# Keys of two row tiles as a seven-product block, and a new order around it, in a PE-bound gated pair of linear attentions

## The chip, the cores and the metric

The kernel runs on one core of a Trainium2 chip. Five engines work side by side, each through its own list of instructions: PE (matmuls into the accumulators in PSUM), DVE and ACT (elementwise work, DVE also sums of two tensors), POOL, and SP, which here issues DMAs. They meet only through semaphores. The metric is device time in microseconds of one execution; the median of three runs of the kernel before is 176.27 us.

## The reference

One input x (2048 rows, 640 columns) goes through two linear attentions A and B with their own weights, and a gate mixes the results:

```python
def branch(x, wqkv, wo):                      # 32 heads of 20
    q, k, v = split(x @ wqkv)
    phi = lambda t: where(t > 0, t + 1, exp(t)) + 1e-6
    pq, pk = phi(q), phi(k)
    kv = einsum("bhsd,bhse->bhde", pk, v)
    z = einsum("bhsd->bhd", pk)
    num = einsum("bhqd,bhde->bhqe", pq, kv)
    den = einsum("bhqd,bhd->bhq", pq, z)[..., None] + 1e-6
    return merge_heads(num / den) @ wo
g = sigmoid((x * gate_w).sum(-1, keepdims=True))
out = g * branch(x, A_wqkv, A_wo) + (1 - g) * branch(x, B_wqkv, B_wo)
```

All tensors are bf16; sums are made in float32.

## The kernel before

**Stages.** The 2048 rows are 16 row tiles of 128, the 640 columns five chunks of 128. The work goes through these stages, each a set of PE products with elementwise work behind it:

- *K, keys.* For every tile t and branch X, `k_step` multiplies the transposed tile by X's key weights, chunk after chunk: five chunks of one 512-wide and one 128-wide matmul (lines 635 and 636), into a pair of PSUM banks. The gate's column rides along as column 640 of B. `k_post` makes phi: ACT takes exp (line 681), DVE clips it (684), and then either ACT takes a relu (693, 708) and DVE adds (699 for both branches at once, 711 for one), or DVE does relu and add in one scalar-tensor-tensor from PSUM (720). The results, pk, lie in PKS, by group of columns and by even and odd tile.
- *G.* In place of values first, the kernel forms pk-transposed times x, and folds the value weights in later (kv). A unit g of five covers two groups of columns, and the sum over rows is split into a 2x2 block product: the rows of even and odd tiles, the left and right 320 columns of x. It is done with seven products, P1 to P7, in place of eight, each over the eight pairs of tiles (line 1029). Tokens Gg.n name product n of unit g: 1 and 2 need only pk and x; 5, 6, 3, 7, 4 need sums that DVE makes ahead: the S sums over pk (`s_pair`, line 761), for four tiles at a time, and the T sums over x (`t_all`, line 786). ACT saves partial results (1058), DVE combines them (c11 and its like, 1063), and SP moves the finished halves by transposing DMAs (`move`).
- *Q and R, queries* (`qu_unit` line 910, `qp_unit` line 997). The first half of the rows, and one unit of the second, again by seven products per group of columns, with weight sums (`w_sums`, 857; `w_sum3`, 868) and x sums (`x_sums`, 883); token X2 makes those of the second half. The lists QD and RD say which phi of a query is finished by one scalar-tensor-tensor of DVE in place of a relu of ACT and an add of DVE.
- *kv, w, LA, d:* kv products (1176), their fold into the output weights (`wp_burst`, 1208) with a trip through DRAM (LA loads A's), and the denominators (`den`, 1282), which go through ACT and small DMAs to scale pq.
- *S, T1, O, output* (1349, 1363, 1418): sums over pq and the folded weights, and seven products for each of eight pairs of row tiles, then stores by SP.

**Order.** Every step is recorded as an operation with its buffers. PE's order is written out by hand as the tokens of MAIN, behind the K stage, which runs through its tiles in a loop. A planner (`Sched`) then walks through time with assumed costs and, for the other engines, takes whatever operation can start first, and of those the one recorded earliest; some have fixed priorities. It gives out the slots: eight PSUM banks (a key unit takes a pair), six exp buffers `ek`, and others. What runs on the chip is the fixed order that comes out, with waits on semaphores. HOP and TURN are such assumed costs: a hop between engines, and the turn of PE between full-array products and those that use a part of the array (kv, w and d have modes 3, 2 and 1).

The K stage before ends with this loop (tiles 0 and 1 come first, in a form of their own):

```python
    for t in range(2, NT):
        k_both(t, "AB" if t in RELUB else "A")
        if t % 2:
            s_pair(t // 2)
    t_all(0, 8)
```

`s_pair` does nothing at even arguments; at 1, 3, 5, 7 it makes the sums of tiles 0 to 3, 4 to 7, 8 to 11 and 12 to 15, the last split into unit 0 and units 1 to 4.

Of the kernel before, what the change touches and what calls it, by code (L numbers as in the profile page):

```python
# [7 lines left out]
ALU = mybir.AluOpType  # L8
# [39 lines left out]
MAIN = """G0.1 G1.1 G2.1 G1.2 G3.1 G2.2 G0.2 G1.5 G0.5 G1.6 G0.6 G1.3 G0.3 G2.5 G1.7 G2.6 G0.7 G2.3 G2.7 G0.4  # L48
G1.4 Q1.1 Q0.1 Q1.5 G2.4 Q0.2 Q0.5 Q0.6 G3.2 G3.5 Q0.3 G3.6 Q0.7 Q1.6 Q1.3 G3.3 Q2.5 G3.7 Q1.7 Q2.1
Q1.2 Q0.4 Q2.2 G3.4 Q2.6 Q3.1 Q4.1 Q4.5 Q2.3 Q1.4 Q3.2 Q4.6 Q2.7 G4.1 Q2.4 Q4.2 Q3.5 Q4.3 Q4.7 Q3.6  # L50
G4.2 G4.5 Q3.7 G4.6 Q4.4 Q3.3 Q3.4 G4.7 kvA X2 G4.3 G4.4 dA0 wA0 R1B wA1 LA dB0 S1 S0
kvB R2A wB0 R1A R3B R4A wB1 T1 R4B R0.1 R0.5 R2B R3A R0.2 R0.6 O0.1 O0.5 O3.1 O2.5 R0.7
R0.3 O0.2 O3.2 O2.1 O3.5 R0.4 O0.6 O3.6 O0.3 O3.3 O2.6 O2.2 O3.7 O1.1 dA1 dB1 S2 S3 O0.7 O2.3
O2.7 O1.2 O1.6 O0.4 O1.5 O1.7 O2.4 O4.1 O5.1 O7.1 O3.4 O1.4 O4.2 O5.2 O7.2 O5.5 O6.1 O5.6 O4.5 O6.2
O6.6 O5.7 O4.6 O5.3 O6.5 O7.6 O4.3 O4.7 O7.5 O7.7 O4.4 O7.3 O6.7 O5.4 O1.3 O6.3 O6.4 O7.4"""
# [5 lines left out]
QD = ("0.0A0", "0.1A0", "0.1B0", "0.2A0", "0.2B0", "0.3A0", "0.4B0", "0.4B1",)  # L61
RD = ("A1", "B0",)
# [38 lines left out]
TURN = 100.0  # L101


class Sched:
# [16 lines left out]
    def run(self):  # L121
# [30 lines left out]
        while len(self.order) < n:  # L152
            best = None
            for e in self.ENGS:
                cand = todo[e]
                if not cand:
                    continue
                look = cand[:1] if e == "PE" else cand
                pick = None
                for o in look:  # L160
                    w = can(o, at[e])
                    if w is None:
                        continue
                    key = (w if w > at[e] + 1e-6 else at[e], o.prio, w)
                    if pick is None or key < pick[0]:
                        pick = (key, o)
                if pick and (best is None or pick[0][0] < best[0][0]):
                    best = (pick[0], pick[1], e)
            if best is None:
                raise RuntimeError("stuck: " + ", ".join(c[0].name for c in todo.values() if c))  # L170
            (w, _, _), o, e = best
            for b in o.outs:
                if b.pool and b.slot is None:
                    self.take(b, w)
            for b in o.outs:
                o.deps += b.war
            w = max(w, at[e])
            if e == "PE" and o.mode != mode:
                w, mode = w + TURN, o.mode
# [24 lines left out]
    def pick(self, b, t, skip=()):  # L204
# [15 lines left out]
        c = [(max(have[i] for i in range(s, s + b.n)), s) for s in b.at if all(i in have for i in range(s, s + b.n))]  # L220
# [83 lines left out]
def body(nc, A_x, A_wqkv, A_wo, B_x, B_wqkv, B_wo, gate_w, out, log=None):  # L304
# [64 lines left out]

    PP = {("A", 0): PQ0[:, :, :].rearrange("p (b g) s -> p g b s", b=2), ("B", 0): PKS[:, 2560:7680].rearrange("p (b g s) -> p g b s", b=2, g=NC)}  # L370
# [13 lines left out]
    OST = {"os": [PKS[:, 8192 + D * k : 8832 + D * k] for k in range(NOS)], "ot": [PKS[:, SSB + D * k : SSB + D * k + D] for k in range(NOT)]}  # L384
# [12 lines left out]
    XU = {k: PKS[:, SSB + 1024 * i : SSB + 1024 * i + 1024].rearrange("p (c s) -> p c s", c=2) for i, k in enumerate((1, 2, 4))}  # L397
    XU[5, 0], XU[5, 1] = PKS[:, 1280:1792], PKS[:, 7680:8192]
# [24 lines left out]
    def dma(q, name, dst, src, nbytes, ins=(), outs=(), after=(), issue=450.0, transpose=False, prio=None, rate=330.0):  # L423
        timing = (rate, 1500.0 if loading else 1700.0) if not transpose else (140.0, 1500.0) if loading else (1000.0, 1150.0)
# [56 lines left out]
    bxo = Buf("xo")  # L481
# [254 lines left out]

    bs1, bs2, bs3, bs4 = [{} for _ in range(4)]
# [108 lines left out]
    gtx = dma("SP", "gtx", GTX.rearrange("p (t n) -> p t n", t=8), GGX, 262144, ins=[bx], outs=[bgt], after=pk_last[-12:], issue=2500.0, transpose=True)
# [23 lines left out]
    def x_sums(p, after):  # L870
        t1, t2 = 1024 * p, 1024 * p + 512
        a11, a12, a21, a22 = [XT[:, c : c + 2, lo : lo + 512] for lo in (t1, t2) for c in (0, 2)]
        for k, in0, in1, need in (
            (1, a21, a22, ()),
            (2, a11, XU[1], (1,)),
            (5, XT[:, 4, t1 : t1 + 512], XT[:, 4, t2 : t2 + 512], ()),
            (4, a12, XU[2], (2,)),
# [5 lines left out]
                lambda e, out=XU.get((k, p), XU.get(k, a21)), in0=in0, in1=in1: e.tensor_tensor(out=out, in0=in0, in1=in1, op=ALU.subtract),  # L883
# [3 lines left out]
                after=after,  # L887
# [8 lines left out]
    def qu_unit(p, g):  # L896
# [33 lines left out]
        def post(X, h, pv, ins):  # L930
# [7 lines left out]
            home = {("B", 0): lambda: [ulast[1]], ("A", 0): lambda: [], ("B", 1): lambda: list(qpe[0]), ("A", 1): lambda: qpe[0] + pqs_op["A", 0] + pqs_op["A", 1] + fx_op[2] + ([ulast[3]] if h else [])}[X, p]()  # L938
# [23 lines left out]
        def step(n):  # L962
# [6 lines left out]
            elif n == 5:  # L969
                mm(pz, True, [(WU[1][:, c, g::5], XU[1][:, c, :]) for c in range(2)] + [(wq("B", 4), xt(4, 1))], wqs + [bwu[1], bxu[p, 1]])  # L970
                d[5] = save(s5, pz)
            elif n == 6:
                mm(px, False, [(WU[2][:, c, g::5], XU[2][:, c, :]) for c in range(2)], [bwu[2], bxu[p, 2]], [d[1]])
                d[2] = save(s2, px)
            elif n == 3:
                mm(pz, False, [(wq("B", 2 + c), XU[4][:, c, :]) for c in range(2)] + [(wq("B", 4), XU[5, p])], wqs + [bxu[p, 4], bxu[p, 5]], [d[5]])
# [12 lines left out]
    def qp_unit(X, g):  # L989
        ps, eq, rq, e2, pq = Buf("q", "ps", 2, cover=(512, 512)), Buf("eq", "eq", 2, (0, 2, 4)), Buf("rq"), Buf("eq2"), Buf("pq")  # L990
        dst = PP[X, 1][:, g, :, :]
        home = list(qpe[0]) + ([ulast[3]] + pqs_op["A", 0] + pqs_op["A", 1] + fx_op[2] if X == "A" else [])
# [31 lines left out]
    def prod(g, name, ps, reg, mov, w, first, ins, after=()):  # L1024
        for j0, j1 in ([(j, j + 1) for j in range(8)] if g == 0 else [(0, 8)]):
# [13 lines left out]
    def g_unit(g):  # L1039
# [8 lines left out]
        ekfree = pk_last[-12:]  # L1048
# [8 lines left out]
        def save(dst, ps, w, name):  # L1057
            return op("ACT", lambda e: e.activation(PT[:, dst.slot, 0:w], PS[:, ps.slot, 0:w], ACT.Copy), act_cost(w), ins=[ps], outs=[dst], after=ekfree, name=name)  # L1058
# [36 lines left out]
        def move(X, k, b):  # L1095
# [9 lines left out]
                after=[gtx] if X == "B" else [],  # L1105
# [5 lines left out]
        def step(n):  # L1111
            if n == 1:
                prod(g, "P1", px, ra1, xv(0, False), W, True, lambda j: xn(j, 0) + [bpk[one[0], 2 * j]])
                d["s1"] = save(t1, px, HC, "p1s")
            elif n == 2:
                prod(g, "P2", py, ra2, xv(1, False), HC, True, lambda j: xn(j, 1) + [bpk[one[0], 2 * j + 1]])
# [143 lines left out]
    def wp_load(X, halves, lo, hi):  # L1260
# [8 lines left out]
            after=[ulast[3]] if X == "A" else [],  # L1269
# [222 lines left out]
    qsteps = []  # L1492
    for tok in MAIN.split():
        if tok[0] == "G":
            g, n = int(tok[1]), int(tok[3])
            steps[g](n)
            if n == 4:
                if g == 0:
                    w_sums([ulast[0]])
                    x_sums(0, [ulast[0]])  # L1500
# [14 lines left out]
        elif tok == "X2":  # L1515
            x_sums(1, qpe[0] + kva)
# [60 lines left out]
```

## Time and profile before

| | |
|---|---|
| runs shown | 175.95, 176.27, 176.41 us |
| the profiled execution's own time | 176.08 us |
| its span, first to last instruction | 174.6 us |
| busy: PE, DVE, ACT, POOL | 171.1, 135.6, 114.2, 5.1 us |
| granted PE clock | 1.00 |
| K products end, first G product starts | 47.8 us |
| DVE's first idle time after the S and T sums | 60.1 us |

The profile lists busy time per engine, the chain of work that ended last, groups of instructions by line, and can be asked for an order in time, for waits, and for busy time in chosen stretches. A matmul's shown length holds its pipeline, so neighbours overlap, and what one costs in a stream is the distance from start to start. A line of a group reads: line, engine, operation, output from inputs, shape, count, busy time, mean length in ns, idle time of the engine ahead of it. An idle PE is what lengthens the span here; idle time of the others need not.

### The profile page before, as it was taken

What the parts mean: (1) busy time and instruction counts of PE and PEld (TensorE: products, weight loads), DVE (VectorE), ACT (ScalarE), POOL (GpSimd) and SP (SyncE); (2) the same over time, 40 slices, a digit from 0 to 9 for tenths busy, and PEclk for the clock granted to TensorE, in tenths of its full rate; (3) what the DMA queues carried; (4) which work ended last, traced back from release to release, by engine and by line L of the source; (5) the groups of instructions that cost most, each with busy time, mean ns of one, the idle gap of its engine ahead of it and who ended that gap; (6) DMA issues with size and microseconds to landing.
All of it is one profiled execution on the core that took longest, in us unless ns stands there. A gap on an engine that the chain in (4) does not pass through costs nothing.

```text
span 174.6 us, 3344 instructions
## 1 busy us (share of the span) xinstructions
PE 171.1 (98%) x1320; PEld 108.0 (62%) x1335; DVE 135.6 (78%) x238; ACT 114.2 (65%) x218; POOL 5.1 (3%) x16
## 2 busy tenths in 40 slices
PE   9999999999999999999999999999999999999995
PEld 5555555555577767666655666655556667777773
DVE  2275996999999755846868879999999995898342
ACT  5378888988841221648699793867899865566332
POOL 2000000000000520000000000000000000000000
PEclk9999999999999999999999999999999999999999
DMA  6979999980000083554261001467670021450135
GB/s 198 295 142 195 190 374 364 350 158 6 4 0 0 0 71 82 99 130 101 41 184 41 0 4 39 97 187 185 243 188 18 0 75 33 92 192 0 38 122 179
DMA packets 33035, 20.59 MB, mean 118 GB/s; under 512 B 18260, under 2 KB 32892, under 8 KB 33020
## 3 DMA queue, kind: packets, MB, share of 16 engines
q1 hardware_dynamic: 32062, 19.76, 44.3%
q10 hardware_dynamic: 958, 0.63, 1.1%
q8 instruction: 10, 0.16, 0.4%
q14 instruction: 5, 0.04, 0.1%
HBM read 10.88 MB, written 4.26 MB: 87 GB/s over the span
## 4 chain that ended last, share of the span: by engine, by line
PE 90%; DVE 6%; ACT 2%; issue 1%; DVEq 0%
PE ps L1418 22%; PE ps L635 19%; PE ps L1029 19%; PE ps L910 12%; PE ps L997 9%; PE ps L636 6%; PE ps L562 1%; DVE WVA L1223 1%; ACT EQ L940 1%; DVE PKS L883 1%; PE ps L1282 1%; PE ps L1208 1%; PE ps L575 1%; DVE WKW L1063 1%; ACT PQ L943 1%
## 5 line engine op out<-in xcount | busy, mean ns | idle before, releaser
L635 PE MATMUL ps<-WKW,XT 128*128 128x512 bf16 x154 | 43.2, 382 | 0.0
L636 PE MATMUL ps<-WKW,XT 128*128 128x128 bf16 (+1 forms) x160 | 35.2, 220 | 0.3
L635 PEld LDWEIGHTS ps<-WKW,XT 128*128 128x128 bf16 x160 | 15.7, 98 | 19.1 <-DMA WKW<-in_A_wqkv_dram 0.3
L681 ACT ACTIVATE EKT<-ps 128x640 bf16<-128x640 f32 x32 | 22.4, 705 | 6.5 <-PE ps L636 5.8
L1029 PE MATMUL ps<-TX,PKS 128*128 128x321 bf16 (+1 forms) x160 | 23.8, 300 | 0.0
L1029 PEld LDWEIGHTS ps<-TX,PKS 128*128 128x128 bf16 x160 | 15.6, 98 | 7.2 <-DVE DEN L1077 0.3
L1029 PE MATMUL ps<-XN,PKS 128*128 128x321 bf16 (+1 forms) x120 | 17.7, 300 | 0.0
L1058 ACT ACTIVATE EKT<-ps 128x321 f32<-128x321 f32 (+1 forms) x15 | 6.4, 440 | 14.9 <-PE ps L1029 8.8
L636 PEld LDWEIGHTS ps<-WKW,XT 128*128 128x128 bf16 x160 | 15.8, 98 | 0.0
L1029 PEld LDWEIGHTS ps<-XN,PKS 128*128 128x128 bf16 x120 | 11.6, 98 | 5.2
L761 DVE TENSOR_TENSOR PKS<-PKS 128x1280 bf16<-128x1280 bf16 (+2 forms) x20 | 13.1, 686 | 0.1
L684 DVE TENSOR_SCALAR EKT<-EKT 128x1280 bf16<-128x1280 bf16 (+1 forms) x18 | 8.2, 454 | 5.9 <-ACT EKT L681 5.7
L940 ACT ACTIVATE EQ<-ps 128x512 bf16<-128x512 f32 x18 | 11.1, 614 | 2.1 <-DVE ps L924 1.4
L1063 DVE TENSOR_TENSOR WKW<-ps,EKT 128x320 bf16<-128x320 f32 x15 | 7.3, 490 | 6.4 <-PE ps L1029 5.8
L1008 ACT ACTIVATE EQ<-ps 128x1024 bf16<-128x1024 f32 x8 | 8.2, 1024 | 3.3 <-PE ps L997 2.6
L720 DVE SCALAR_TENSOR_TENSOR PKS<-ps,EKT 128x640 bf16<-128x640 f32 x12 | 9.9, 821 | 0.1
L910 PE MATMUL ps<-XT,WQA 128*128 128x512 bf16 x34 | 9.5, 379 | 0.1
L997 PE MATMUL ps<-XT,WQA 128*128 128x512 bf16 x37 | 9.0, 380 | 0.3 <-DVE PKS L1304 0.2
L997 PE MATMUL ps<-XT,WQB 128*128 128x512 bf16 x39 | 9.1, 380 | 0.2 <-issue 0.2
L693 ACT ACTIVATE PKS<-ps 128x640 bf16<-128x640 f32 x12 | 8.4, 698 | 0.0
L953 DVE TENSOR_SCALAR EQ<-EQ 128x512 bf16<-128x512 bf16 (+1 forms) x19 | 6.0, 322 | 2.7 <-ACT EQ L940 2.7
L1441 DVE TENSOR_TENSOR PKS<-ps,PKS 128x320 bf16<-128x320 f32 x8 | 3.9, 490 | 5.2 <-PE ps L1418 5.2
(155 smaller groups left out, 307.3 us busy)
## 6 DMA issues: line engine op xcount, KB each, us to landing
out_dram<-PKS SPq DMA_DIRECT2D x15, 160.0 KB, 1.8
XN<-in_A_x_dram SPq DMA_DIRECT2D x1, 2240.0 KB, 9.3
WKW<-in_A_wqkv_dram SPq DMA_DIRECT2D x5, 160.0 KB, 3.8
WKW<-in_B_wqkv_dram SPq DMA_DIRECT2D x5, 160.0 KB, 3.9
WQA<-in_A_wqkv_dram SPq DMA_DIRECT2D x1, 800.0 KB, 10.9
WQB<-in_B_wqkv_dram SPq DMA_DIRECT2D x1, 800.0 KB, 13.7
WVA<-in_A_wqkv_dram SPq DMA_DIRECT2D x1, 800.0 KB, 12.5
PKS<-in_B_wqkv_dram SPq DMA_DIRECT2D x1, 800.0 KB, 5.0
```

Of the source, the lines that this page charges most:

```text
L635: e.matmul(a[:, 0:512], l, WK[X][:, c, 0:512], start=(c == 0), stop=(c == NC - 1))
L636: return e.matmul(a[:, 512:w], l, WK[X][:, c, 512:w], start=(c == 0), stop=(c == NC - 1))
L681: op("ACT", lambda e, i=i, ps=ps: e.activation(evg(i), psg(ps), ACT.Exp), act_cost(D), ins=[ps] + first, outs=[ek, b], name="ke")
L693: op("ACT", lambda e, X=X, ps=ps: e.activation(pkt(X, t), psg(ps), ACT.Relu), act_cost(D), ins=[ps], outs=[rk], name="kr")
L720: lambda e, X=X, i=i, ps=ps: e.scalar_tensor_tensor(pkt(X, t), psg(ps), 0.0, evg(i), op0=ALU.max, op1=ALU.add),
L761: lambda e: e.tensor_tensor(out=out, in0=a, in1=b, op=ALU.subtract),
L910: r = e.matmul(PS[:, ps.slot, :], w, x, start=(first and i == 0), stop=(i == len(prs) - 1), skip_group_check=not first)
L940: o = [op("ACT", lambda e: e.activation(EQ[:, eq.slot + h, :], pv(), ACT.Exp), act_cost(512), ins=ins, outs=[eq], name="qe")]
L997: r = e.matmul(PS[:, ps.slot + h, :], WQ[X][:, c, g::5], XT[:, c, 1024 + 512 * h : 1536 + 512 * h], start=(c == 0), stop=(c == NC - 1))
L1029: r = e.matmul(PS[:, ps.slot, 0:w], reg[:, j, :], mov(j, w), start=(first and j == 0), stop=(j == 7), skip_group_check=not first)
L1063: lambda e: e.tensor_tensor(out=GT[:, dst.slot, lo : lo + HC], in0=PS[:, ps.slot, 0:HC], in1=PT[:, src.slot, 0:HC], op=ALU.add),
L1418: r = e.matmul(PS[:, ps.slot, 0:HALF], reg(g), mov(g), start=(first and g == 0), stop=(g == NC - 1), skip_group_check=not first)
```

## The change

**The block.** The keys of tiles 12 and 13 (KU = 6) of both branches become one 2x2 block product: rows are the two tiles, columns the two branches, and the sum runs over chunks 0, 1 against 2, 3 (chunk 4 is added in plain form). `ks_unit` has seven steps, K6.1 to K6.7, with 2, 3, 3, 2, 3, 2, 3 chunks for n = 1, 2, 5, 6, 3, 7, 4. It holds three pairs of banks: px, py, pz. ACT copies the first product from px to py (the fork), and saves two more into float buffers `kq`; DVE adds a saved one back in twice (`kcm`). DVE makes four weight sums ahead (`kw_sums`, 2 x 641 elements, recorded behind tile 4) and five sums of transposed x (`kx_sums`, behind tile 9). A memset on POOL makes column 640 of A's weights zero.

**Around it.** The loop over tiles stops at 9 (KT = 10). Tiles 10, 11, 14, 15 become tokens KtX, one branch of one tile each, and stand in MAIN between the block's steps; KRS lists which of these units take their relu on ACT. After the last K token, `after_k` records the sums of tiles 12 to 15 and the gate's operations, which now also wait for the last key product on PE.

**First sums in two parts.** P1 and P2 of a G unit are cut at KJ = 7: tokens 1 and 2 sum over the first seven pairs of tiles, tokens 8 and 9 over the last (tiles 14 and 15), with the save and the combine behind these.

**New order.** MAIN is new throughout. Among others, kvA and X2 stand among the Q steps, some forty tokens ahead of wA0 (X2's sums have buffers of their own and only one of them waits for kvA), dA0 comes behind wA0 in place of ahead of it, and QD and RD give DVE one more Q half and two more R units. A few buffers move (A's folded weights, the output staging), A's load of them waits for all Q steps and the last G unit, and the planner's assumed time for transposing DMAs and for one kind of turn changes.

```diff
-MAIN = """G0.1 G1.1 G2.1 G1.2 G3.1 G2.2 G0.2 G1.5 G0.5 G1.6 G0.6 G1.3 G0.3 G2.5 G1.7 G2.6 G0.7 G2.3 G2.7 G0.4
...
-G4.2 G4.5 Q3.7 G4.6 Q4.4 Q3.3 Q3.4 G4.7 kvA X2 G4.3 G4.4 dA0 wA0 R1B wA1 LA dB0 S1 S0
...
+KT = 10
+KU = 6
+KJ = 7
+KRS = ("10A", "10B", "11A", "11B", "12A", "13B", "14A", "14B", "15A", "15B", "8A", "9A", "9B",)
+MAIN = """K14A K6.1 K10A K6.2 K6.5 K6.6 K14B K6.3 K10B K6.7 K11A K11B K6.4 K15A K15B G2.1 G1.1 G2.8 G0.1 G3.1
+G1.8 G0.2 G0.8 G0.9 G1.2 G2.2 G2.9 G3.2 G0.6 G0.5 G1.9 G0.7 G3.8 G1.6 G0.3 G2.6 G1.5 G1.7 G0.4 G2.5
+G1.3 Q1.1 G2.7 G1.4 Q1.2 Q1.5 Q1.6 G3.9 G3.6 G2.3 Q1.7 Q1.3 Q0.1 Q1.4 Q4.5 Q4.1 Q0.2 Q0.6 Q0.5 G2.4
+Q4.6 Q4.2 Q0.7 kvA X2 Q0.3 G4.1 Q4.3 G4.2 G3.5 Q0.4 G4.8 Q4.7 G3.7 Q2.5 G3.3 Q2.1 G3.4 Q3.1 Q2.6
+Q2.3 G4.5 Q2.7 G4.6 Q4.4 Q2.2 G4.7 Q3.6 Q3.5 Q3.2 Q3.7 Q2.4 G4.9 G4.3 Q3.4 G4.4 Q3.3 wA0 dA0 R1A
+wA1 LA dB0 S1 S0 kvB R4A wB0 R2B R4B R1B wB1 T1 R3B R0.1 R3A R2A R0.6 R0.5 O1.1
...
+O7.2 O7.3 O7.4"""
...
-QD = ("0.0A0", "0.1A0", "0.1B0", "0.2A0", "0.2B0", "0.3A0", "0.4B0", "0.4B1",)
-RD = ("A1", "B0",)
+QD = ("0.0A0", "0.0A1", "0.1B0", "0.1B1", "0.2A0", "0.2B0", "0.2B1", "0.3A0", "1.0B1",)
+RD = ("A0", "A1", "A4", "B0",)
...
-TURN = 100.0
+TURN, TURNS = 100.0, {(1, 2): 190.0}
...
+    def kw_sums():
+        a1, a2, b1, b2 = [WK[X][:, c : c + 2, 0 : D + 1] for X in XS for c in (0, 2)]
+        for k, in0, in1, how, need in ((1, b1, a1, ALU.subtract, ()), (2, kw(1), b2, ALU.add, (1,)), (3, b1, b2, ALU.add, ()), (4, a2, kw(2), ALU.subtract, (2,))):
...
+                dve2(1282),
...
+        def step(n):
+            if n == 1:
+                mm(px, D + 1, True, [(WK["A"][:, c, :], xt(c, 0)) for c in range(2)], bx + [bwk["A", c] for c in range(2)] + [bwz])
+                d[1] = op("ACT", lambda e: e.activation(psw(py, D), psw(px, D), ACT.Copy), act_cost(D), ins=[px], outs=[py], name="kfk")
+            elif n == 2:
+                mm(py, D, False, [(WK["A"][:, c, :], xt(c, 0)) for c in range(2, 5)], bx + [bwk["A", c] for c in range(2, 5)])
+            elif n == 5:
+                mm(pz, D + 1, True, [(KW[1][:, c, :], KX[1][:, c, :]) for c in range(2)] + [(WK["B"][:, 4, :], xt(4, 1))], bx + [bkw[1], bkx[1], bwk["B", 4], bgc])
+                d[5] = save(s5, pz, D + 1)
+            elif n == 6:
+                mm(px, D + 1, False, [(KW[2][:, c, :], KX[2][:, c, :]) for c in range(2)], [bkw[2], bkx[2]], [d[1]])
+                d[2] = save(s2, px, D + 1)
+            elif n == 3:
+                mm(pz, D + 1, False, [(WK["B"][:, 2 + c, :], KX[4][:, c, :]) for c in range(2)] + [(WK["B"][:, 4, :], KX[5])], [bkx[4], bkx[5], bgc] + [bwk["B", c] for c in range(2, 5)], [d[5]])
+                comb(pz, s2, False)
+                k_post(t1, [("A", py, "%dA" % t1 in KRS), ("B", pz, "%dB" % t1 in KRS)])
+            elif n == 7:
+                mm(px, D + 1, False, [(KW[3][:, c, :], KX[3][:, c, :]) for c in range(2)], [bkw[3], bkx[3]], [d[2]])
+                d[7] = comb(px, s5, True)
+            elif n == 4:
+                mm(px, D, False, [(KW[4][:, c, :], xt(2 + c, 1)) for c in range(2)] + [(WK["A"][:, 4, :], xt(4, 1))], bx + [bkw[4], bwk["A", 4]], [d[7]])
+                for X, ps in (("B", s5), ("A", px)):
+                    k_post(t2, [(X, ps, "%d%s" % (t2, X) in KRS)])
...
-    for t in range(2, NT):
+    for t in range(2, KT):
         k_both(t, "AB" if t in RELUB else "A")
         if t % 2:
             s_pair(t // 2)
+        if t == 4:
+            kw_sums()
     t_all(0, 8)
...
+    kx_sums()
...
-            if n == 1:
-                prod(g, "P1", px, ra1, xv(0, False), W, True, lambda j: xn(j, 0) + [bpk[one[0], 2 * j]])
+            if n in (1, 8):
+                prod(g, "P1", px, ra1, xv(0, False), W, True, lambda j: xn(j, 0) + [bpk[one[0], 2 * j]], js=(0, KJ) if n == 1 else (KJ, 8))
...
-            after=[ulast[3]] if X == "A" else [],
+            after=qpe[0] + [ulast[NPU - 1]] if X == "A" else [],
...
-            x_sums(1, qpe[0] + kva)
+            x_sums(1, lambda k: kva if k == 3 else [ulast[1 if k == 5 else 2]])
```

More of the change, by code (lines that the diff above doesn't have):

```diff
@@ L219, in pick @@
             return best[0], best[4]
-        c = [(max(have[i] for i in range(s, s + b.n)), s) for s in b.at if all(i in have for i in range(s, s + b.n))]
+        c = [(max(have[i] for i in range(s, s + b.n)), s) for s in b.at if all(i in have for i in range(s, s + b.n)) and (not b.need or all(self.cover[s + i] >= b.need[i] for i in range(b.n)))]
         return min(c) if c else None
@@ new lines, in ks_unit, with xt, mm, fn @@
+    def ks_unit(j):
+        px, py, pz = [Buf("k", "ps", 2, cover=(512, 129)) for _ in range(3)]
+        py.need = (512, 128)
+        s2, s5 = [Buf("kq", "kq") for _ in range(2)]
+        d = {}
+        t1, t2 = 2 * j, 2 * j + 1
+        def xt(c, h):
+            return XT[:, c, 256 * j + 128 * h : 256 * j + 128 * h + 128]
+        def mm(ps, w, first, prs, ins, after=()):
+            def fn(e):
+                a = psw(ps, w)
+                for i, (m, l) in enumerate(prs):
+                    for lo, hi in ((0, 512), (512, w)):
+                        r = e.matmul(a[:, lo:hi], l, m[:, lo:hi], start=(first and i == 0), stop=(i == len(prs) - 1), skip_group_check=not first)
+                return r
+            kpe[:] = [op("PE", fn, len(prs) * (mm_cost(512) + mm_cost(128)), ins=ins, outs=[ps], after=after, name="K%d" % j)]
+        def save(dst, ps, w):
+            return op("ACT", lambda e: e.activation(psw(dst, w), psw(ps, w), ACT.Copy), act_cost(w), ins=[ps], outs=[dst], name="ksv")
+        def comb(ps, src, into_src):
+            return op(
+                "DVE",
+                lambda e: e.tensor_tensor(out=psw(src if into_src else ps, D + 1), in0=psw(ps, D + 1), in1=psw(src, D + 1), op=ALU.add),
+                dve1(D + 1),
+                ins=[ps, src],
+                outs=[src if into_src else ps],
+                name="kcm",
+            )
+        bx = [bxt[t1], bxt[t2]]
+        def step(n):
[21 more added lines that the diff above has]
+                    k_post(t2, [(X, ps, "%d%s" % (t2, X) in KRS)])
+        return step
@@ L1047, in g_unit @@
         W = HC + 1
-        ekfree = pk_last[-12:]
         d = {}
```

164 lines of the change are left out of this document (117 added, 47 removed).

## The prediction

> **What bounds the kernel now.** I read the busy totals first, then who waited for whom, then busy time by stage, then the order in time.
>
> ```profile
> PE 171.1 (98%) x1320; PEld 108.0 (62%) x1335; DVE 135.6 (78%) x238; ACT 114.2 (65%) x218; POOL 5.1 (3%) x16
> ...
> PE 90%; DVE 6%; ACT 2%; issue 1%; DVEq 0%
> ```
>
> PE is busy for 98% of the span, and the chain that ended last runs 90% through it. A busy PE may still wait inside its pipeline, so the list of PE's waits is asked too; these are all that it holds:
>
> ```profile
> PE ps L562 <- DVE ONE L461: 0.3, 1, 0.3
> PE ps L997 <- DVE PKS L1304: 0.2, 1, 0.2
> PE ps L997 <- issue: 0.2, 1, 0.2
> ```
>
> 0.3 us of it is the start. PE is a gapless stream, so a matmul that goes saves its whole stream time, and any new wait is paid in full. The stages (columns: length, then PE, PEld, DVE, ACT, POOL busy):
>
> ```profile
> 13.50:31.60 18.10, 17.94 (x132) 10.30 (x134) 14.48 (x24) 15.83 (x30) 0.00 (x0) 1.00 1.05 285
> 31.60:48.00 16.40, 16.29 (x121) 9.29 (x121) 15.98 (x23) 14.52 (x28) 0.00 (x0) 1.00 0.45 115
> 48.00:57.50 9.50, 9.50 (x72) 6.80 (x71) 9.13 (x19) 2.86 (x8) 0.00 (x0) 1.00 0.00 0
> 57.50:72.00 14.50, 14.45 (x104) 10.08 (x103) 9.04 (x21) 3.58 (x9) 3.88 (x4) 1.00 0.43 59
> 72.00:98.00 26.00, 25.89 (x148) 15.84 (x149) 18.01 (x41) 20.95 (x44) 0.34 (x2) 1.00 0.40 93
> 98.00:113.00 15.00, 14.56 (x240) 9.84 (x241) 13.78 (x29) 10.04 (x19) 0.00 (x0) 1.00 0.18 37
> 113.00:131.00 18.00, 17.89 (x106) 9.55 (x108) 17.79 (x27) 14.90 (x19) 0.00 (x0) 1.00 0.71 198
> ```
>
> The second is that of tiles 10 to 15: DVE 97% and ACT 89% full. The third, where DVE finishes the first sums, is as full. Granted clock 1.00 throughout.
>
> **The PE stream.** One chunk of a key product is a 512-wide and a 128-wide matmul; in the order in time they start 0.27 us apart:
>
> ```profile
> 31.76 0.38 PE L635 MATMUL ps<-WKW,XT 128*128 128x512 bf16 x1
> 31.98 0.22 PE L636 MATMUL ps<-WKW,XT 128*128 128x128 bf16 x1
> 32.03 0.38 PE L635 MATMUL ps<-WKW,XT 128*128 128x512 bf16 x1
> ```
>
> Tiles 10 to 15 are 60 chunks from 31.65 to 47.98: 0.272 each. Tiles 12 and 13 need 20 chunks now. The block product has 2+3+3+2+3+2+3 = 18. Saved: 2 x 0.272 = **0.54 us**. Splitting P1 and P2 after seven of eight pairs adds no matmul; those of Q, R, O stay.
>
> The order also swaps dA0 and wA0. Turns between full and part-array matmuls show as longer starts:
>
> ```profile
> 106.81 0.73 PE L1282 MATMUL ps<-PQ,DEN 128*32 128x256 bf16 x20
> 107.56 0.60 PE L1208 MATMUL ps<-WOA,WVA 64*60 64x320 bf16 x15
> 108.35 2.11 PE L997 MATMUL ps<-XT,WQB 128*128 128x512 bf16 x9 [0.18 <-issue]
> 110.38 0.60 PE L1208 MATMUL ps<-WOA,WVA 64*60 64x320 bf16 x15
> 110.92 0.73 PE L1282 MATMUL ps<-PKS,DEN 128*32 128x256 bf16 x20
> 111.58 1.13 PE L1176 MATMUL ps<-GSB,PKS 128*64 128x60 bf16 x55
> ```
>
> A den group followed by a wp burst takes 0.75 us to the next start (106.81 to 107.56), the one followed by kv 0.66. After the swap no den precedes a burst: **0.09 us** saved (bounds 0 and 0.12; I take the difference of the two rows). The 0.18 idle at 108.35 is one of ten matmuls missing from the records (x9), no gain. At most 0.1 more hangs on the gap at 61.87, where PE started 0.24 us later in place of 0.13; I count nothing.
>
> Sum: 0.54 + 0.09 = 0.63 us, against the profiled 176.08 (span 174.6 and 1.5 around it): 175.45. The median shown, 176.27, lies 0.19 higher: **175.64**. Everything else must hide.
>
> **DVE, key stage.** Prices: a bf16 sum of 1280 elements 0.82 (0.74 start to start when queued), of 256 0.29 (0.20), a scalar-tensor-tensor of 640 from PSUM 0.82 (0.73). Float sums from PSUM took 0.49 at 320 and 0.70 at 512, so 641 take some 0.84, 0.76 queued.
> - Four weight sums: 4 x 0.82 = 3.3 us. They need only the weights and come after tile 4 in priority; DVE idles before 31.6 by 0.71 + 0.65 + 1.42 + 0.35 + 1.42 = 4.55 us (gaps at 9.9, 12.9, 15.3, 24.1, 26.2). Five x sums, 4 x 0.2 to 0.3 and a smaller one, some 1.3 us, need transposed tiles 12, 13 and fit the last two gaps. Hidden, 0.3 us carried over. Without the gaps all 4.6 us would stand before the S sums.
> - Two combines: +1.5. Relus in place of scalar-tensor-tensors (10B, 14B, 15B in, 13A out): minus 0.7. Together +0.8 us.
> - Due work from 31.65 until the second S sum of unit 0: rest of tile 8 0.55, S sums of tiles 4 to 7 1.5, carried 0.3, tile 9 1.2, the six tiles and combines 9.35, four T sums 5.6, S sums of tiles 8 to 11 2.9, two of unit 0 0.4, two c11 0.8, waits between dependent operations 0.8 (as they now stand): 23.4, so done at 55.05. The first consumer, G0.6, comes after 8 x 0.94 + 5 x 0.134 = 8.15 us of P1 and P2, from 47.45: at 55.6. Margin **0.5 us**. Bounds: 0 (margin holds), and 1 us of stall where a 1.5 us T sum is put ahead of a due one.
>
> No trace here shows a two-source bf16 sum with odd rows; the weight sums have rows of 641. Bounds: 0.82 (the 1280 row) and, at the float rows' 1.08 ns per element, 0.70 + 770 x 1.08 = 1.53. I take 0.82, the nearest in type and size. [...]
>
> **ACT and PSUM, key stage.** ACT gets the fork into py and two saves (0.70 each, by the 640-wide rows) and two relus more: +3.5 us by durations, +3.1 at the 0.61 from start to start when queued. From tile 10 on: 25 wide operations x 0.61 + six small ones = 16 to 16.5 us against 15.8 of stage. It ends some 0.5 us later than now (48.9): about 49.5; pk of tile 15 at 50.3, first needed by G0.9 at 52.5.
> PSUM has four pairs of banks and the block holds up to three. Stepping the tokens through with these prices: K6.5 starts at 35.7, its pair (14A's) free at 35.0; K14B 37.1, pair free 36.3; K10B 39.3, py free 38.7; K11A 41.2, free 40.1; **K11B 42.53, free 42.35 to 42.45**; K6.4 43.9, combine done 42.0; K15B 46.1, free 43.7. No stall, one margin of about 0.1. Bounds: 0 to 1.6 us (below). Nothing here can gain, for the stream had no wait.
>
> **Later stages.** No DMA is added. kvA moves from 103 us to about 82. Its last transpose follows G2.3, with 7.5 us of Q and G steps between; combine, issue and landing take 0.5 + 1.2 + 2.6 = 4.3 at most with the queue free. On SP the gate's transpose (2.5 issue) stands before some moves, which the 3.2 us left cover. X2's sums, 4 x 0.69 + 0.42 + 0.82 = 4.0 us of DVE, go from 105 to 111 us, where DVE is 92% full, to the stage 72 to 98, where it idles 8 us; two more R units on DVE give 2 x (1.22 - 0.69) = 1.1 back, while ACT is spared 2 us. The A load (LA) now waits for the last Q and G steps, both issued before wA0, and for its stores after wA1 as before: zero. The last store follows O7.4 as before: zero. Edits that only loosen (relus of R's A units 0 and 1 without the first den's DMAs, X2 waiting for kvA in one sum of six) cost nothing; one more memset on POOL at the start, some 0.1 by the 5.1 us that 16 POOL operations take, lies before the first K product beside the loads; the gate's POOL sums now also wait for the last key product, 10 us before they start (58.5). Planner constants and moved buffers issue nothing.
>
> **The rivals.**
> 1. *A late sum.* DVE misses the 0.5 us margin at G0.6, or a step of the reordered 57 to 98 us. Against: about 1.5 us of slack behind G0.6. For: DVE is 97% full before. A stall of 0.1 to 1.1 us gives 175.75 to 176.75; about 176.1 at the middle.
> 2. *The other side: the pairs of PSUM.* ACT falls behind, PE waits for a pair at K11B, again at K15A. It decides once ACT needs its 0.70 us a piece instead of 0.61: 25 x 0.70 + 1 = 18.5 against 15.8 plus the 1 us it may trail, 1.7 us of stall, 176.27 - 0.63 + 1.7 = 177.3. For: margin 0.1. Against: two ACT operations in a row start 0.60 apart at 14.0 and 46.7.
> 3. *Odd rows at single rate.* 4 x 0.71 = 2.8 us that no gap holds; less 0.5 of margin, 2.3 us of stall at G0.6: 177.9.
>
> **How the numbers follow.** Forecast, no stall above 0.1 us: 0.52. Rival 1: 0.29. Rival 2: 0.13. Rival 3, with mishaps of that size elsewhere: 0.06. 0.3% (0.53 us) is about what a measurement of this kernel can tell from no change: faster is below 175.74, slower above 176.80. So faster 0.52, same 0.29, slower 0.19. The likeliest gives 175.6, its own range 175.3 to 175.8 (all turns and the gap at 61.87 gained, and noise of 0.2 as between the runs shown). The range reaches over rival 1: 175.3 to 176.8.
>
> **What would show it.** Right: 316 key matmuls in place of 320, 36 of them under the block's line; first product matmul at 47.4 to 47.5; PE's list of waits still under 1 us; weight sums at 0.82 before 17 us; no den just before a burst. Wrong: PE waiting for ACT in 35 to 46 us (rival 2), for a DVE sum at 55 to 62 (1, 3), weight sums at 1.5 (3), or a PE gap near kvA, 80 to 84, ended by a DMA.

## The result and the profile after

| | before | after |
|---|---|---|
| median | 176.29 us | 176.83 us |
| profiled execution | 176.08 us | 176.63 us |
| its span | 174.6 us | 175.2 us |

The ratio is 1.0028, 95% interval 1.0020 to 1.0036: the changed kernel is slower by 0.49 us (0.35 to 0.63). The interval leaves out 1, so the loss is clear of noise, although it is below the 0.3% that the prediction took for the least that can be told from no change. It lies on the other side of the forecast of 175.6, and the median is 0.03 us past the end of the range. One of the 22 runs of the changed kernel was slow, 257.22 us; it counts in the median and not in the ratio.

The page of the changed kernel gives the busy totals and the chain that ended last:

```profile
PE 172.1 (98%) x1331; PEld 107.6 (61%) x1331; DVE 140.3 (80%) x246; ACT 116.2 (66%) x221; POOL 4.9 (3%) x17
...
PE 94%; ACT 4%; issue 1%; DVE 0%; ACTq 0%
```

PE is as full as before. What is new is the 4% of ACT in the chain, where before it was 6% of DVE and 2% of ACT. The waits of PE in the changed kernel, all of them:

```profile
PE ps L1156 <- ACT PKS L711: 0.3, 1, 0.3
PE ps L580 <- DVE ONE L478: 0.3, 1, 0.3
PE ps L653 <- ACT GE L690: 0.2, 1, 0.2
```

The total is 0.8 us, against 0.7 before, which looks harmless. But two of these are new, one in the first key tiles (line 653) and one in the first products of G (line 1156), and the list counts a wait only from the modelled end of the matmul before. The stages of the changed kernel (length, then busy PE, PEld, DVE, ACT, POOL) point to the second:

```profile
13.50:31.60 18.10, 18.10 (x135) 10.30 (x134) 15.30 (x29) 15.45 (x30) 0.00 (x0) 1.00 1.10 275
31.60:48.00 16.40, 16.40 (x123) 9.29 (x121) 16.08 (x23) 15.47 (x29) 0.00 (x0) 1.00 0.49 127
48.00:57.50 9.50, 9.10 (x66) 6.12 (x65) 8.79 (x19) 4.71 (x10) 0.00 (x0) 1.00 0.00 0
57.50:72.00 14.50, 14.50 (x107) 10.28 (x106) 10.77 (x24) 4.10 (x10) 3.73 (x4) 1.00 0.27 51
```

The third is the only one of these four in which PE isn't full (9.10 of 9.50, before 9.50), and ACT, 2.86 us busy there before, now has 4.71: it is late.

**Where the time went.** The true measure is the distance between starts of matmuls in the order in time. Cut into four stretches at places that all kernels here share, it gives (us, by the starts as printed):

| | tile 2's first key product to the first one behind tile 9 | from there to the first G product | from there to the den group of the second half (dA1) | from there to the last matmul | sum |
|---|---|---|---|---|---|
| before | 21.77 | 16.32 | 96.16 | 28.25 | 162.50 |
| after | 22.13 | 15.79 | 96.69 | 28.25 | 162.86 |
| difference | +0.36 | -0.53 | +0.53 | 0.00 | +0.36 |

The promised saving is there, in its place: 0.53 us of the 0.54. It is given back twice: 0.36 ahead of it, 0.53 behind it. The sum starts at tile 2, since that start itself falls anywhere from 9.72 to 10.52 us in executions of kernels that do the same until then; with that, +0.36 agrees with the +0.49 (0.35 to 0.63) of the runs, at the low end of the interval.

**The first place: tile 3.** PE in the changed kernel:

```profile
12.56 0.22 PE L654 MATMUL ps<-WKW,XT 128*128 128x129 bf16 x1
12.99 0.38 PE L653 MATMUL ps<-WKW,XT 128*128 128x512 bf16 x1 [0.21 <-ACT GE L690]
```

After a narrow matmul the next starts 0.055 us on; here it is 0.43. The loss is 0.375 us, of which the bracket shows 0.21. The first key product of tile 3 waits for a pair of PSUM banks. What DVE did just before, in the changed kernel:

```profile
9.17 0.82 DVE L767 TENSOR_TENSOR GSA<-WKW 128x1282 bf16<-128x1282 bf16 x1
9.91 0.81 DVE L738 SCALAR_TENSOR_TENSOR PKS<-ps,EKT 128x640 bf16<-128x640 f32 x1
10.64 0.82 DVE L767 TENSOR_TENSOR GSA<-GSA,WKW 128x1282 bf16<-128x1282 bf16 x1
11.38 0.32 DVE L702 TENSOR_SCALAR EKT<-EKT 128x640 bf16<-128x640 bf16 x1
11.61 0.82 DVE L767 TENSOR_TENSOR GSB<-WKW 128x1282 bf16<-128x1282 bf16 x1
12.35 0.82 DVE L738 SCALAR_TENSOR_TENSOR PKS<-ps,EKT 128x640 bf16<-128x640 f32 x1
```

All four weight sums (line 767) stand among the scalar-tensor-tensors of tiles 0 and 1, each of which is the last to read a pair of banks and so frees it; three of the sums stand ahead of the third, shown last here. In the kernel before, the third began at 11.02:

```profile
11.02 0.82 DVE L720 SCALAR_TENSOR_TENSOR PKS<-ps,EKT 128x640 bf16<-128x640 f32 x1
```

It begins at 12.35 now; 0.18 of the difference is the later start of tile 2 in this trace. In the order before, tile 3 took the pair that this operation frees; the planner, with the pair late, gave it that of tile 2's branch A, which a relu of ACT frees at 12.84:

```profile
12.13 0.71 ACT L726 ACTIVATE PKS<-ps 128x640 bf16<-128x640 f32 x1
```

Either way PE waits: the other pair comes free at 13.17. The bracket names line 690, the gate's exp, but that one ends at 12.99, after the weight load of the late matmul has begun (12.96), so it is not what PE waited for.

**The second place: the start of G.** ACT in the changed kernel, end of the key stage:

```profile
45.13 0.71 ACT L699 ACTIVATE EKT<-ps 128x640 bf16<-128x640 f32 x1
45.71 0.21 ACT L690 ACTIVATE GE<-PQ 128x1 f32<-128x1 f32 x1
45.81 1.40 ACT L726 ACTIVATE PKS<-PQ 128x640 bf16<-128x640 f32 x1
47.08 1.40 ACT L699 ACTIVATE EKT<-PQ 128x640 bf16<-128x640 f32 x1
48.34 1.33 ACT L699 ACTIVATE EKT<-ps 128x640 bf16<-128x640 f32 x2
49.50 0.22 ACT L690 ACTIVATE GE<-ps 128x1 f32<-128x1 f32 x1
49.55 0.77 ACT L711 ACTIVATE PKS<-ps 128x640 bf16<-128x640 f32 x1
50.14 0.78 ACT L699 ACTIVATE EKT<-ps 128x640 bf16<-128x640 f32 x1
50.72 0.79 ACT L711 ACTIVATE PKS<-ps 128x640 bf16<-128x640 f32 x1
```

Relu and exp of unit 13B take 1.40 us each; the same operation on the same 640 floats takes 0.71 from PSUM. 13B is the one key unit whose floats lie in SBUF: the block's combine leaves them in s5, a buffer in PQ. Both kinds of read go through `psg`, which takes every fifth element (20 bytes on) to put the columns in order of groups. From start to start the two cost 1.27 and 1.26 in place of some 0.6, so the relus of 15A and 15B (line 711) end at 50.32 and 51.51. First PE at the start of G in the kernel before, in one piece, then in the changed kernel, with its weight loads, which show the second wait better:

```profile
47.81 7.80 PE L1029 MATMUL ps<-XN,PKS 128*128 128x321 bf16 x56
```

```profile
48.77 1.26 PE L1156 MATMUL ps<-XN,PKS 128*128 128x321 bf16 x8
50.37 2.32 PE L1156 MATMUL ps<-XN,PKS 128*128 128x321 bf16 x14 [0.34 <-ACT PKS L711]
...
51.56 0.52 PEld L1156 LDWEIGHTS ps<-XN,PKS 128*128 128x128 bf16 x5 [0.39 <-ACT PKS L711]
```

G0.1 starts at 50.37, right behind the first relu, G3.1 at 51.56, right behind the second: both products were given the banks that these relus free. By starts they are 0.51 and 0.225 us late, 0.735 together. Against it stand the turn (0.10) and the gap at 61.87, which is gone (0.11): 0.735 - 0.10 - 0.11 = 0.53, as in the third column of the table.

### The profile page after: what moved, and what is told of

The parts are those of the page before. It is cut to its first block, busy times and chain, and to the rows that moved or that the text cites. A ratio compares the mean times of both kernels' runs of the same rounds, so it can differ in the third digit from the quotient of the medians.

```text
span 175.2 us, 3364 instructions
## 1 busy us (share of the span) xinstructions
PE 172.1 (98%) x1331; PEld 107.6 (61%) x1331; DVE 140.3 (80%) x246; ACT 116.2 (66%) x221; POOL 4.9 (3%) x17
## 4 chain that ended last, share of the span: by engine, by line
PE 94%; ACT 4%; issue 1%; DVE 0%; ACTq 0%
PE ps L1546 22%; PE ps L1156 20%; PE ps L653 16%; PE ps L1035 13%; PE ps L1124 10%; PE ps L654 4%; ACT EKT L699 3%; PE ps L809 3%; PE ps L580 1%; PE ps L1410 1%; PE ps L1336 1%; PE ps L1304 1%; ACT PKS L711 1%; PE ps L593 1%; ACT PKS L726 0%
## 5 line engine op out<-in xcount | busy, mean ns | idle before, releaser
L653 PE MATMUL ps<-WKW,XT 128*128 128x512 bf16 x140 | 39.5, 383 | 0.2 <-ACT GE L690 0.2
L654 PE MATMUL ps<-WKW,XT 128*128 128x128 bf16 (+1 forms) x140 | 30.9, 221 | 0.0
L699 ACT ACTIVATE EKT<-ps 128x640 bf16<-128x640 f32 x31 | 21.6, 711 | 5.3 <-PE ps L654 4.8
L653 PEld LDWEIGHTS ps<-WKW,XT 128*128 128x128 bf16 x140 | 13.8, 99 | 17.2 <-issue 0.7
L1156 PE MATMUL ps<-XN,PKS 128*128 128x321 bf16 (+1 forms) x120 | 18.7, 300 | 0.4 <-ACT PKS L711 0.3
L654 PEld LDWEIGHTS ps<-WKW,XT 128*128 128x128 bf16 x140 | 13.8, 99 | 0.0
L711 ACT ACTIVATE PKS<-ps 128x640 bf16<-128x640 f32 x16 | 11.4, 711 | 0.0
L1035 PE MATMUL ps<-XT,WQA 128*128 128x512 bf16 x36 | 10.4, 379 | 0.0
L1124 PE MATMUL ps<-XT,WQA 128*128 128x512 bf16 x40 | 9.2, 381 | 0.0
L1611 ACT ACTIVATE PKS<-ps 128x320 bf16<-128x320 f32 x8 | 3.5, 437 | 8.1 <-PE ps L1546 8.1
L738 DVE SCALAR_TENSOR_TENSOR PKS<-ps,EKT 128x640 bf16<-128x640 f32 x10 | 8.2, 818 | 0.0
L1569 DVE TENSOR_TENSOR PKS<-ps,EKT 128x320 bf16<-128x320 f32 x9 | 4.4, 491 | 4.1 <-PE ps L1546 3.8
```

The source lines that it names most:

```text
L653: e.matmul(a[:, 0:512], l, WK[X][:, c, 0:512], start=(c == 0), stop=(c == NC - 1))
L654: return e.matmul(a[:, 512:w], l, WK[X][:, c, 512:w], start=(c == 0), stop=(c == NC - 1))
L699: op("ACT", lambda e, i=i, ps=ps: e.activation(evg(i), psg(ps), ACT.Exp), act_cost(D), ins=[ps] + first, outs=[ek, b], name="ke")
L711: op("ACT", lambda e, X=X, ps=ps: e.activation(pkt(X, t), psg(ps), ACT.Relu), act_cost(D), ins=[ps], outs=[rk], name="kr")
L738: lambda e, X=X, i=i, ps=ps: e.scalar_tensor_tensor(pkt(X, t), psg(ps), 0.0, evg(i), op0=ALU.max, op1=ALU.add),
L1035: r = e.matmul(PS[:, ps.slot, :], w, x, start=(first and i == 0), stop=(i == len(prs) - 1), skip_group_check=not first)
```

## The experiments

The theory after the traces: two separate causes, the weight sums early on DVE (0.36 us) and the strided reads of SBUF on ACT (0.7 us). The rivals: that both gaps are only ACT carrying more work, or that the reads are slow because the buffer is in SBUF at all, however it is read. Kernels that stand in one table shared the runs of the kernel before.

| | edit of | median | ratio to before |
|---|---|---|---|
| e1_late_w | after | 176.27 | 0.9994 (0.9981 to 1.0007) |
| e9_swap | after | 181.45 | 1.0283 (1.0266 to 1.0300) |
| e2_flat13 | after | 175.94 | 0.9972 (0.9961 to 0.9984) |
| e8_no13B | after | 176.32 | 0.9992 (0.9980 to 1.0004) |

### e1_late_w: the weight sums later

```diff
+        if t == 2:
+            kw_after = [pk_last[-1]]
...
                 ins=[bwk[X, c] for X in XS for c in range(4)] + [bgc, bwz] + [bkw[j] for j in need],
                 outs=[bkw[k]],
+                after=kw_after,
```

> The four weight sums may start only once the keys of tile 2 are done; all else is as in the changed kernel. Theory (a): the changed kernel loses 0.4 us at 12.6 because the sums stand on DVE ahead of the scalar-tensor-tensors of tiles 0 and 1, which free PSUM. Then PE goes on without the 0.38 us gap there, the first G product starts at 47.4 in place of 47.8, and the ratio to before falls from 1.0028 to about 1.0005 (176.4). Rival: the gap belongs to the start (clock, first loads) and stays; ratio 1.0028.

Measured 0.9994 against 1.0028, the expected 1.0005 within the interval. DVE in this kernel:

```profile
12.40 0.82 DVE L738 SCALAR_TENSOR_TENSOR PKS<-ps,EKT 128x640 bf16<-128x640 f32 x1
...
15.74 0.83 DVE L767 TENSOR_TENSOR GSA<-WKW 128x1282 bf16<-128x1282 bf16 x1
16.49 0.83 DVE L767 TENSOR_TENSOR GSB<-WKW 128x1282 bf16<-128x1282 bf16 x1
```

The sums come behind the last scalar-tensor-tensor of the first tiles, at the same price, and tile 3 starts without a gap: from tile 2 to the first key product behind tile 9 it takes 21.76 us, as in the kernel before (21.77). Nothing later on DVE came too late for it. The waits at the start of G stay (0.50 and 0.22 by starts), so the causes are two.

### e2_flat13: 13B read in order

```diff
         def psg(ps):
+            if ps.pool == "kq":
+                return psw(ps, D).rearrange("p (g m) -> p g m", g=NC)
             return psw(ps, D).rearrange("p (m g) -> p g m", g=NC)
```

> As in the changed kernel, but the exp and relu of tile 13, branch B, read and write in order; the permutation of its columns is left out, so keys of this tile and branch stand at the wrong columns. It tells the read's stride from the place. Theory (b): 0.70 each, no PE gap at 49 to 52, ratio about 0.9986. If reading float32 from SBUF costs 1.4 us in any order, times and gaps stay. Rival (ACT overloaded as such): gaps above 0.4 us stay.

Measured 0.9972, a little better than the 0.9986 expected, which lies outside the interval; in the traces, from tile 2 on, it is 0.75 us below the changed kernel, as expected. ACT in this kernel, and PE from the start of G:

```profile
46.35 0.75 ACT L728 ACTIVATE PKS<-PQ 128x640 bf16<-128x640 f32 x1
46.97 0.74 ACT L701 ACTIVATE EKT<-PQ 128x640 bf16<-128x640 f32 x1
...
48.35 8.47 PE L1158 MATMUL ps<-XN,PKS 128*128 128x321 bf16 x61
```

From the same buffer in SBUF, in order, 0.75 and 0.74 in place of 1.40. So it isn't SBUF as such, and it isn't the stride as such either, since the same stride in PSUM takes 0.71: what is dear is the 20-byte stride in SBUF, at 1.40. The first 61 matmuls of G run in one piece: both later waits are gone, with as many operations on ACT as in the changed kernel, so ACT was not overloaded as such. The wait of tile 3 stays (0.377 us, behind the matmul at 13.10).

### e9_swap: read in order, written with a stride

```diff
         def psg(ps):
+            if ps.pool == "kq":
+                return psw(ps, D).rearrange("p (m g) -> p m g", g=NC)
             return psw(ps, D).rearrange("p (m g) -> p g m", g=NC)
...
+        def mg(ps, v):
+            return v.rearrange("p g m -> p m g") if ps.pool == "kq" else v
...
-            op("ACT", lambda e, i=i, ps=ps: e.activation(evg(i), psg(ps), ACT.Exp), act_cost(D), ins=[ps] + first, outs=[ek, b], name="ke")
+            op("ACT", lambda e, i=i, ps=ps: e.activation(mg(ps, evg(i)), psg(ps), ACT.Exp), act_cost(D), ins=[ps] + first, outs=[ek, b], name="ke")
```

> The exp and relu of tile 13, branch B, read their float buffer in SBUF in order and write with a stride, where the changed kernel reads with a stride and writes in order. Same instructions in the same order. Theory (b): it is the strided read of float32 from SBUF that doubles these two (1.40 us each in place of 0.70), and the 1.4 us that ACT is late makes the two PE gaps at 49.7 and 51.2 (0.51 and 0.23). Then they take about 0.70, both gaps go, ratio about 0.9986. If a strided write costs the same, they stay at 1.4 and the ratio at 1.0028. Rival: ACT is late through its added operations as such (3.5 us more work); then the gaps stay above 0.4 us even at 0.70.

This was expected to mend the loss (0.9986) and made it far worse: 1.0283. ACT in this kernel, in order of time:

```profile
45.77 3.07 ACT L731 ACTIVATE PKS<-PQ 128x640 bf16<-128x640 f32 x1
48.33 3.35 ACT L704 ACTIVATE EKT<-PQ 128x640 bf16<-128x640 f32 x1
```

Neighbouring bf16 elements now go to places 256 bytes apart in the exp buffer (line 704, 3.35 us) and, by the layout of PKS, 4096 bytes apart for the relu (line 731, 3.07 us). The longest of PE's waits in this kernel, and the stretches around it (length, busy PE, PEld, DVE, ACT, POOL, granted clock):

```profile
PE ps L1161 <- ACT PKS L716: 3.5, 1, 3.5
```

```profile
50.00:54.30 4.30, 0.79 (x6) 0.59 (x7) 2.00 (x5) 4.30 (x7) 0.00 (x0) 1.00 0.00 0
54.30:57.40 3.10, 3.10 (x14) 1.53 (x13) 3.10 (x5) 1.12 (x3) 0.00 (x0) 0.51 0.00 0
57.40:64.00 6.60, 6.60 (x49) 4.70 (x48) 4.96 (x12) 1.09 (x4) 0.00 (x0) 0.97 0.00 0
```

PE waits 3.5 us for the relu of 15A, and then pays again: for 3.1 us from 54.3 on the clock is granted at 0.51, and over the 6.6 us behind at 0.97, together some 1.7 us of full clock (0.49 x 3.1 + 0.03 x 6.6). The waits of up to 0.5 us in the changed kernel left the clock at 1.00; what a wait between these lengths does is not shown.

### e8_no13B: DVE reads the stride in place of one ACT operation

```diff
-KRS = ("10A", "10B", "11A", "11B", "12A", "13B", "14A", ...
+KRS = ("10A", "10B", "11A", "11B", "12A", "14A", ...
```

> The relu of tile 13, branch B, goes from ACT to DVE (a scalar-tensor-tensor from the float buffer in place of relu and add). Theory (b): ACT is spared the 1.39 us relu, exp stays at 1.4, so ACT is late by 0.7 less than its 1.4; the gap at 49.7 falls below 0.1, that at 51.2 as well, unless the sum on DVE is slowed by the same stride: 0.82 us if not, 1.2 or more if it is. Ratio 0.999 to 1.001. Rival (ACT overloaded as such): same direction, gap smaller by up to 0.7, so this run tells prices and not the cause.

Measured 0.9992. Without 13B in the list its relu goes from ACT to a scalar-tensor-tensor of DVE. ACT and DVE in this kernel:

```profile
46.39 1.40 ACT L699 ACTIVATE EKT<-PQ 128x640 bf16<-128x640 f32 x1
...
49.03 1.31 DVE L738 SCALAR_TENSOR_TENSOR PKS<-PQ,EKT 128x640 bf16<-128x640 f32 x1
50.26 0.82 DVE L738 SCALAR_TENSOR_TENSOR PKS<-ps,EKT 128x640 bf16<-128x640 f32 x1
```

DVE pays here too, 1.31 us against 0.82 with the same stride in PSUM, 0.77 ns more an element. No run lets this operation read the buffer in order; the block's combine, which adds 641 floats read in order from such a buffer to as many from PSUM, took 0.82 to 0.83 in the changed kernel, so on DVE too the stride in SBUF is the likely cause. One slow read less on ACT shortens the waits at the start of G from 0.735 to 0.27 us. I had expected under 0.1 to be left: the exp alone still makes ACT too late.

The second set of kernels, with its own runs of the kernel before (e14_swap_d was run once, beside its profile):

| | edit of | median | ratio to before |
|---|---|---|---|
| e13_late_m129 | after | 175.67 | 0.9953 (0.9937 to 0.9970) |
| e15_w_alone | before | 176.98 | 1.0031 (1.0018 to 1.0044) |
| e14_swap_d | before | 176.82 (one run) | |

### e13_late_m129: both mends

```diff
         def psg(ps):
+            if ps.pool == "kq":
+                return psw(ps, 645).rearrange("p (g m) -> p g m", g=NC)[:, :, 0:128]
...
+        def gm(b):
+            return psw(b, 645).rearrange("p (g m) -> p g m", g=NC) if b.pool == "kq" else psw(b, 645).rearrange("p (m g) -> p g m", g=NC)
...
-                d[5] = save(s5, pz, D + 1)
+                d[5] = save_gm(s5, pz)
...
-                d[7] = comb(px, s5, True)
+                d[7] = comb_gm(px, s5)
```

and `after=kw_after`, which in e1_late_w holds the weight sums back. The save into s5 and the combine do the permutation themselves, while they read PSUM, and write five runs of 129 floats (128 columns and, in the first, the gate's); exp and relu then read s5 in order.

> Both mends at once, with every column in its place: the weight sums start after the keys of tile 2, and the save of product 5 writes its float buffer by column groups (645 columns read from PSUM with a stride, written in order), so that the combine, the exp and the relu of tile 13, branch B, go through SBUF in order. Theory (a) and (b) together: no PE gap of the three is left, so the stream's saving of 0.54 and the turn's 0.1 come through: ratio 0.9955 to 0.9970, 175.6 to 175.9 against 176.4. If the strided read of PSUM with a float32 write costs ACT more than 0.75 us, K6.3 or K11B waits. Rival (ACT overloaded as such): gaps at 48 to 52 us come back, ratio 0.998 to 1.000.

Measured 0.9953, a little beyond the expected 0.9955 to 0.9970: faster than the kernel before by 0.83 us (0.53 to 1.11). Its trace, tile 2 to the end, is 161.75 us, 0.75 below. ACT and PE in order of time, then the third stage, then all of PE's waits:

```profile
45.58 0.75 ACT L731 ACTIVATE PKS<-PQ 128x640 bf16<-128x640 f32 x1
46.20 0.74 ACT L704 ACTIVATE EKT<-PQ 128x640 bf16<-128x640 f32 x1
...
47.58 8.47 PE L1173 MATMUL ps<-XN,PKS 128*128 128x321 bf16 x61
```

```profile
48.00:57.50 9.50, 9.50 (x72) 6.84 (x70) 9.15 (x20) 3.49 (x9) 0.00 (x0) 1.00 0.00 0
```

```profile
PE ps L653 <- DMA WKW<-in_A_wqkv_dram: 0.5, 2, 0.3
PE ps L580 <- DVE ONE L478: 0.3, 1, 0.3
```

No wait is left behind the first loads, and G is one piece again. The moved permutation is free on ACT: the save took 0.729 us with the stride in PSUM, that of the other partial result, in order, 0.736. By columns it is 21.77, 15.78, 95.95 and 28.25: the 0.54 of the block, and 0.21 of turn and vanished gap.

### e15_w_alone: the sums put into the kernel before

```diff
+    op("POOL", lambda e: e.memset(WKC[:, :, 0, D : D + 1], 0.0), 100.0, outs=[bwz], name="wkz")
...
+        if t == 4:
+            kw_sums()
```

The four weight sums and the memset of a column; nothing reads them.

> The kernel before with nothing added but the four weight sums (and the memset of their column) recorded behind tile 4; nobody reads them. Theory (a): they are put ahead of the same scalar-tensor-tensors, and PE gets the gap of 0.38 us at about 12.6 with no block in the program at all: ratio 1.0015 to 1.003. Rival (the gap belongs to the block's or the start's other changes): no gap, ratio 1.000.

Measured 1.0031, and the same gap. PE in this kernel:

```profile
13.19 0.22 PE L638 MATMUL ps<-WKW,XT 128*128 128x129 bf16 x1
13.62 0.38 PE L637 MATMUL ps<-WKW,XT 128*128 128x512 bf16 x1 [0.21 <-ACT GE L674]
```

0.43 from start to start again, 0.375 lost. From tile 2 to the first key product behind tile 9 it takes 22.14 us, the rest is that of the kernel before. The sums alone (with the small memset on POOL) bring the first loss; no block is needed for it.

### e14_swap_d: the swap alone in the kernel before

```diff
-G4.2 G4.5 Q3.7 G4.6 Q4.4 Q3.3 Q3.4 G4.7 kvA X2 G4.3 G4.4 dA0 wA0 R1B wA1 LA dB0 S1 S0
+G4.2 G4.5 Q3.7 G4.6 Q4.4 Q3.3 Q3.4 G4.7 kvA X2 G4.3 G4.4 wA0 dA0 R1B wA1 LA dB0 S1 S0
```

> The kernel before with dA0 and wA0 exchanged and nothing else. The turn theory of the prediction: from the start of the first den group to the next start 0.66 us in place of 0.75, from the burst's start to the next 0.54, PE stream shorter by about 0.1 us; the time itself can't show that in one look. Rival: the longer turn has to do with the first use of a part of the array and not with the pair den, burst; then it moves to the burst.

176.82 in one run, no gain. In its trace the burst (line 1208) is followed by the den group (1282) 0.66 us on, in place of the 0.54 expected:

```profile
107.30 0.60 PE L1208 MATMUL ps<-WOA,WVA 64*60 64x320 bf16 x15
107.96 0.73 PE L1282 MATMUL ps<-PQ,DEN 128*32 128x256 bf16 x20
```

The den group waits 0.13 us there for an operation of DVE on DEN, which eats the turn. In the changed kernel DEN is ready, and the same two rows stand closer:

```profile
107.47 0.60 PE L1336 MATMUL ps<-WOA,WVA 64*60 64x320 bf16 x15
108.00 0.73 PE L1410 MATMUL ps<-PQ,DEN 128*32 128x256 bf16 x20
```

0.53. So the turn's 0.10 us is real, but it is the whole new order that earns it, not the swap. The rival, a longer turn that moves to the burst, is out: the burst starts 0.23 us behind the 320-wide matmul ahead of it, as the den group did in the kernel before. A further 0.23 of the swapped kernel's time is a wait of PE for a relu of ACT at 128.8, which the changed kernel doesn't have; the swap also moved some later operations in the planner's order, and no run tells which of them brought the wait.

## Why the prediction was wrong

By its own steps:

- **The PE stream, 0.54: right.** 280 matmuls under the tile's lines and 36 under the block's, 316 in all, and 0.53 us less from the end of tile 9 to G. The sign named for it, the first G product at 47.4 to 47.5, didn't show (47.82), because of the loss ahead of it.
- **The turn, 0.09: right.** 0.10. The gap at 61.87, counted at nothing with at most 0.1 hanging on it, went: 0.11 more, a gain outside the sum.
- **"Four weight sums ... Hidden": wrong, 0.36 us.** The sum over DVE's gaps (4.55 us of idle time against 3.3 + 1.3) was right, and proved nothing. The planner takes what can start first; a sum that needs only weights goes in as soon as DVE has nothing ready, and if that is just ahead of a scalar-tensor-tensor, it pushes it back by up to 0.82, the length of a sum. I named no operation queued behind the sums, though the view of DVE in time showed at 11.02 the one that frees tile 3's banks. e1_late_w and e15_w_alone show it from both sides.
- **ACT, "25 wide operations x 0.61": wrong, 0.735 us.** I priced by width alone. Two of the 25 read floats in SBUF with a stride, and cost 0.65 us more each, 1.3 us of lateness: ACT's last relu, of 15B, ended at 51.5, where I had 49.5. With those two in order (e13_late_m129) it ended at 49.98 in a trace whose tile 2 starts 0.31 later than before, so the rest of this sum was sized right. And pk, which I had at 50.3, wasn't the first to matter: the banks that 15A and 15B hold were needed by G0.1 and G3.1, ahead of G0.9, which I took as the first consumer. Rival 2 had engine and resource right, an ACT that falls behind and PE that waits for a pair, and place, cause and price wrong: pieces from PSUM still started 0.6 apart, K11B and K15A had no wait, and the price was 0.74 in place of 1.7.
- **Margin at G0.6, odd rows: right.** PE has no gap from 51.6 to 62, so rival 1 didn't happen. There the late start of G had given DVE 0.735 us more, but e13_late_m129, where G isn't late, has no gap either. (8 x 0.94 + 5 x 0.134 is 8.19 and not 8.15; the margin doesn't hang on it.) The price of the weight sums, 0.82, was an estimate from the row of 1280; with rows of 641 they took 0.82 each, so rival 3, whose "single rate" is the 1.08 ns an element of the float rows (1.53 for a sum), is dead.
- **Later stages at zero: right.** kvA at 83 us, X2's sums and LA bring no wait, and from dA1 on both kernels take 28.25 us. The memset on POOL was priced at some 0.1 us from 5.1 us for 16 operations, which is 0.32 each; in the trace it took 0.12 (line 499), and no wait of PE shows it.

In one line: -0.53 of stream, -0.10, -0.11, against +0.36 and +0.735, makes +0.36 in the traces. Without the two mis-sized terms it would have been -0.75, which is what e13_late_m129 shows. That the median lies only 0.03 us past the range is luck: the range was stretched to 176.8 for rival 1, which didn't happen, and two other losses filled it.

The stride is a price of the layout: elements 20 bytes apart in SBUF took 1.40 us against 0.75 in order on ACT, and 1.31 against 0.82 from PSUM on DVE. These runs show the price and not its mechanism.

What stays open: why the same stride costs ACT and DVE nothing in PSUM is not settled by these runs, only that it is so (0.71 for ACT, against 0.70 of the fork's copy in order; 0.82 for DVE, as of the combine in order). The layouts between, strides of two to four floats, were not tried.

## What to carry to other kernels

Where PE has no gaps, spare time on another engine hides an added operation only if no operation that stands behind it in the fixed order frees what PE waits for (here four sums of 0.82 us cost 0.36): look at the neighbours in time, not at the sum of the gaps. Price a copy or an activation by its operands' memory and stride, not by its width alone (here 0.71 from PSUM with the stride, 0.75 from SBUF in order, 1.40 from SBUF with the stride); when float32 columns must be permuted as here, do it at the operation that reads PSUM (0.729 us with the stride, 0.736 in order), and leave SBUF in order. A list of waits can look the same while 1.1 us are lost: compare the starts of matmuls stage by stage.

## What the runs showed of the hardware

| 640 floats to bf16 | us |
|---|---|
| ACT, PSUM, 20-byte stride | 0.71 |
| ACT, SBUF, in order | 0.74 to 0.75 |
| ACT, SBUF, 20-byte stride | 1.40 |
| ACT, SBUF in order, bf16 written to SBUF 256 bytes apart | 3.35 |
| ACT, SBUF in order, bf16 written to SBUF 4096 bytes apart | 3.07 |
| DVE scalar-tensor-tensor, PSUM, 20-byte stride | 0.82 |
| DVE scalar-tensor-tensor, SBUF, 20-byte stride | 1.31 |

The two strided writes, 3.07 and 3.35 us, were by far the dearest of them; I had expected them to be as cheap as the read in order. And one wait of 3.5 us cost PE a second time, through 3.1 us at a granted clock of 0.51 (e9_swap).
